# Recurrence output written in place in slots of 32 partitions, two units loaded ahead into the second activation tile, own tile for r*u*k

## The chip, the cores and the metric

One Trainium2 chip, one of its cores. The metric is the device time of one execution in microseconds (us), of which the median of several runs is given.

## What is computed

A recurrence per batch and head, and behind it two dense layers with their own activations:

```python
for t in range(S):                       # B, H, S, D = 4, 8, 768, 48
    cur = einsum('bhd,bhe->bhde', u * k[t], v[t])
    y[t] = einsum('bhd,bhde->bhe', r[t], state + cur)
    state = w[t][..., None] * state + einsum('bhd,bhe->bhde', k[t], v[t])
x = y as (3072, 384)
h = x @ w_in;  g = h - tanh(h);  x = g @ w_out          # 384 -> 2048 -> 384
h = x @ w_in2; s = h * softmax(h); x = layernorm(s) * g_ln @ w_out2   # 384 -> 1024 -> 384
```

The weights come as float64 and are converted on the chip into a high and a low part of f32 (tiles wa, wb); each dense product is three matmuls, low times high, high times low and high times high.

## The kernel before

**Recurrence.** The sequence of a batch is cut into NC = 6 chunks of 128 steps; batch times chunk gives 24 units. A unit is worked in stages: att_load (DMAs of w, r, k into rkw[u % 2], of v into vt[u % 4]), att_pre (range check of w on ScalarE, ACT; r*u*k on GpSimd, POOL; its sum per head on VectorE, DVE), att_0 (transposes of w and r on TensorE, PE; running product, scans of L274), att_1 (k scaled, L286 to L288), att_2 (q·k on PE, L301, masked into aq by L303; kt, the transpose of k), att_3 (state update: ds on PE, L317 and L318; st on DVE), att_4 (y). The heads stand in pairs j = 0..3: head 2j on partitions 0 to 47, head 2j+1 on 64 to 111.

In att_4, y of pair j lies in p[:, j] on the same partitions: 48 rows of each head, 16 left free. There are two calls with the state (L340, not in the first unit of a sequence) and two with aq (L343) per pair. Pairs 0 to 2 are copied (high part by ACT, L345, low part by DVE, L347) into the activation tile xs of the block; pair 3 goes to x3 (L346, L348) and from there by six DMAs (L351) into the free rows of xs. load_w1 puts the rows of w_in in the same order by four DMAs.

r*u*k is written to self.ruk, which is a view of inv; inv is also written by L286 and read by L288.

**Dense layers.** Six blocks of 512 columns (four units each), 16 steps m in each: part1 (L381, nine matmuls into hp, then the activation on ACT, DVE, POOL) and, two steps later, part2 (L405, nine matmuls into x2p). In block 0 each step also converts a pair of weight tiles (conv_a: raw loads by load_w1 and load_w2, then L121 to L135; two raw tiles in turn). xs[0] and xs[1] serve the blocks in turn. Then comes the third layer (L462, L544), which the change doesn't touch.

**Order.** The kernel writes work in a chosen order: a list `first` of stages of units 0 to 3 and of the first two conversions, sorted by keys (stage number plus 2.1 per unit), and then one loop over the steps s of all blocks, into which the later units' stages are placed. A planner orders the instructions of each engine's queue by that order as priority and by its own estimate of when each is ready; every queue then runs in its order. All DMAs are issued by SyncE (SP).

Of the kernel before, what the change touches and what calls it, by code (L numbers as in the profile page):

```python
# [20 lines left out]
C = 128  # L21
NC = S // C
# [36 lines left out]
class Kern:  # L59
# [101 lines left out]
    def att_setup(self, att, xp0, xp1):  # L161
        nc = self.nc
        rkw = att.tile([128, 2 * 3 * H * 64 + 32], F32, name="rkw")
        self.rkw = [x.rearrange("p (i h d) -> p i h d", i=3, h=H) for x in (rkw[:, 0:RKW], rkw[:, RKW:2 * RKW])]
        self.grp = [rkw[:, ROW * i:ROW * (i + 1) + 32] for i in range(3)]
        self.nat = rkw[:, 3 * ROW + 32:2 * RKW + 32].rearrange("p (i h d) -> p i h d", i=2, h=H)
        self.vt = [att.tile([128, DM], F32, name=f"vt{i}") for i in range(4)]
        self.inc = [att.tile([128, 4, C + 1], F32, name=f"inc{i}") for i in range(2)]
        self.rh = [att.tile([128, 4, C], F32, name=f"rh{i}") for i in range(2)]
        self.kh = [att.tile([128, 4, C], F32, name=f"kh{i}") for i in range(2)]  # L170
        self.inv = att.tile([128, 4, C], F32, name="inv")
        self.aq = att.tile([128, 2, 4, C], F32, name="aq")
# [12 lines left out]
        for t in self.st:
            nc.gpsimd.memset(t, 0.0)

    def att_load(self, u):
        nc = self.nc
        b, c = divmod(u, NC)  # L190
        t = self.rkw[u % 2]
# [3 lines left out]
        nc.sync.dma_start(  # L195
            out=self.vt[u % 4].rearrange("p (h d) -> p h d", h=H),
            in_=self.v[b, :, sl, :].rearrange("h p d -> p h d"),
        )

# [10 lines left out]
    def load_turned(self, u):  # L210
# [7 lines left out]
        for i, src in ((0, self.r), (1, self.k)):  # L218
            nc.sync.dma_start(out=self.nat[:, i], in_=src[b, :, sl, :].rearrange("h p d -> p h d"))
        nc.sync.dma_start(  # L220
            out=self.vt[u % 4].rearrange("p (h d) -> p h d", h=H),
            in_=self.v[b, :, sl, :].rearrange("h p d -> p h d"),
        )
        self.load_grp(0, u)
# [12 lines left out]
    def att_pre(self, u):  # L237
        nc = self.nc
        t = self.rkw[u % 2]
# [5 lines left out]
        nc.vector.reduce_sum(self.dg[u % 2].rearrange("p e j -> p j e"), self.ruk.rearrange("p (j e) d -> p j e d", e=2), axis=AX)  # L245

# [63 lines left out]
    def att_3(self, u):  # L310
# [5 lines left out]
        for j in range(4):  # L316
            self.mm(p[0:64, j], kn[:, j, 0:64], vt[:, 2 * j * D:2 * j * D + D], start=True, stop=True)  # L317
            self.mm(p[64:NP, j], kn[:, j, 64:NP], vt[:, (2 * j + 1) * D:(2 * j + 2) * D], start=True, stop=True)  # L318
        old, new, inc = self.st[u % 2], self.st[(u + 1) % 2], self.inc[u % 2]
        for e in range(2):  # L320
            s = slice(64 * e, 64 * e + D)
            n = new[s, :, s]
            end = inc[s, :, C:C + 1].to_broadcast([D, 4, D])
            if u % NC == 0:
                v.tensor_tensor(n, p[s], end, ALU.mult)
            else:
                v.tensor_tensor(n, p[s], old[s, :, s], ALU.add)
                v.tensor_tensor(n, n, end, ALU.mult)

    def att_4(self, u):  # L330
# [242 lines left out]
def fast_path(tc, K, const):  # L573
# [108 lines left out]
def general_path(tc, K, const):  # L682

    nc, v = tc.nc, tc.nc.vector
    with tc.tile_pool(name="g_dram", bufs=1, space=bass.MemoryType.DRAM) as dram:
# [23 lines left out]
        with (  # L709
# [166 lines left out]
```

## Time and profile before

| what | value |
|---|---|
| median of 3 runs | 778.8 us (777.76 to 779.06) |
| profiled execution, own time | 782.14 us |
| its span, first to last instruction | 780.3 us |
| mean granted clock of PE | 0.985 |
| PE busy | 731.3 us, 94% of the span |
| DVE busy | 582.5 us, 75% |
| ACT busy | 495.0 us, 63% |
| POOL busy | 419.7 us, 54% |
| DMA queue of the kernel | 112.19 MB, 55.5% of 16 engines' span |

Busy time is that of instructions under way, and matmuls overlap each other, so a busy PE is not PE at its peak. A wait is put down to the operation that came last. Times of rows are from the start of the span.

### The profile page before, as it was taken

The page shows a single profiled execution, that of the slowest core. Times are in us where ns is not written, and L with a number is a line of the kernel's source. Part 1 is how long each engine was busy: PE and PEld are TensorE (multiplying, and loading weights), DVE is VectorE, ACT ScalarE, POOL GpSimd, SP SyncE. Part 2 cuts the span into 40 slices and gives each one's busy share as a digit, 9 for nine tenths or more (in the row PEclk, how much of TensorE's full clock was granted, in tenths as well). Part 3 has the DMA queues.
Part 4 walks back from the last instruction along what each step waited for, and adds up shares of the span by engine and source line. Part 5 has one row for each costly group of instructions (what it writes and reads, how often), then busy time and mean ns, then how long its engine had stood idle before and what let it go on. Part 6 is the DMA issues. An engine that isn't in the chain of part 4 may idle for free. (4 is left out here: it accounts for less than half of the span.)

```text
span 780.3 us, 13211 instructions
## 1 busy us (share of the span) xinstructions
PE 731.3 (94%) x4338; PEld 605.5 (78%) x4338; DVE 582.5 (75%) x1023; ACT 495.0 (63%) x944; POOL 419.7 (54%) x389
## 2 busy tenths in 40 slices
PE   3677989899999999999999999999999999999996
PEld 2565767678887888887887887887778999998986
DVE  4688989776776677766676765468569899999992
ACT  3434777487776777686777765697745554554552
POOL 3444657466565656646555655367425444545440
PEclk9978999999999999999999999999999999999999
DMA  9964674778587568657665630043035555645531
GB/s 164 184 101 116 132 179 122 169 176 206 127 182 184 137 152 184 172 145 205 158 158 162 178 88 25 25 143 121 5 130 184 178 172 168 195 161 171 184 108 46
DMA packets 178158, 113.12 MB, mean 145 GB/s; under 512 B 95520, under 2 KB 166816, under 8 KB 178080
## 3 DMA queue, kind: packets, MB, share of 16 engines
q1 hardware_dynamic: 178080, 112.19, 55.5%
q8 instruction: 36, 0.59, 0.3%
q14 instruction: 42, 0.34, 0.1%
HBM read 88.81 MB, written 20.97 MB: 141 GB/s over the span
## 5 line engine op out<-in xcount | busy, mean ns | idle before, releaser
L405 PE MATMUL x2p<-g,wa 128*128 128x512 f32 x864 | 223.9, 398 | 4.0 <-ACT g L395 2.8
L381 PE MATMUL hp<-xs,wa 128*128 128x512 f32 x864 | 216.9, 395 | 5.5 <-DVE y L392 5.0
L381 PEld LDWEIGHTS hp<-xs,wa 128*128 128x128 f32 x864 | 162.5, 190 | 43.1 <-POOL wa L135 7.0
L405 PEld LDWEIGHTS x2p<-g,wa 128*128 128x128 f32 x864 | 158.1, 188 | 42.6 <-issue 4.2
L398 POOL TENSOR_TENSOR g<-y,g 128x512 fp32r<-128x512 f32 x96 | 128.6, 1340 | 42.7 <-ACT g L395 33.3
L387 DVE TENSOR_TENSOR y<-hp,t 128x512 f32<-128x512 f32 x96 | 65.9, 687 | 81.3 <-ACT t L386 65.5
L393 ACT ACTIVATE q<-t,cst 128x512 f32<-128x512 f32 x96 | 69.4, 723 | 65.6 <-DVE y L392 65.1
L462 PE MATMUL h<-wb,x2s 128*128 128x512 f32 x432 | 103.8, 392 | 3.0 <-POOL x2s L451 1.4
L544 PE MATMUL o<-wb,ts 128*128 128x384 f32 x576 | 105.1, 336 | 1.0 <-POOL ts L523 1.0
L544 PEld LDWEIGHTS o<-wb,ts 128*128 128x128 f32 x576 | 100.8, 188 | 3.0 <-POOL ts L523 1.3
L462 PEld LDWEIGHTS h<-wb,x2s 128*128 128x128 f32 x432 | 80.6, 188 | 20.0 <-POOL x2s L451 1.9
L397 POOL TENSOR_SCALAR g<-y 128x512 fp32r<-128x512 f32 x64 | 40.3, 630 | 91.9 <-DVE y L392 65.4
L386 ACT ACTIVATE t<-hp 128x512 f32<-128x512 f32 x96 | 56.5, 589 | 26.1 <-PE hp L381 25.4
L523 POOL TENSOR_TENSOR ts<-tw,ts 128x512 fp32r<-128x512 f32 x44 | 57.9, 1339 | 7.5 <-ACT ts L522 7.4
L392 DVE SCALAR_TENSOR_TENSOR y<-q,y 128x512 f32<-128x512 f32 x64 | 49.9, 780 | 4.4 <-ACT q L390 1.2
L451 POOL TENSOR_TENSOR x2s<-x2s 128x384 fp32r<-128x384 f32 x24 | 24.9, 1040 | 49.9 <-ACT x2s L450 49.9
L495 ACT ACTIVATE e<-so 128x1024 f32<-128x1024 f32 x24 | 25.5, 1060 | 37.2 <-DVE so L494 37.2
L390 ACT ACTIVATE q<-t,cst 128x512 f32<-128x512 f32 x64 | 46.2, 722 | 1.2
L519 DVE STREAM_TRANSPOSE tw<-sw 128x1024 f32<-128x1024 f32 x22 | 45.0, 2046 | 2.6 <-DMA sw<-dso 2.4
L286 POOL TENSOR_TENSOR inv<-inc,kh 112x512 f32<-112x512 f32 x24 | 29.7, 1236 | 32.0 <-ACT kh L278 25.9
L135 POOL TENSOR_TENSOR wa<-cv_x,wa 128x768 fp32r<-128x768 f32 x16 | 29.4, 1839 | 29.7 <-ACT wa L134 29.7
L301 PEld LDWEIGHTS qk<-rh,kh 48*128 48x128 f32 x384 | 28.0, 200 | 18.8 <-issue 12.3
(134 smaller groups left out, 1208.1 us busy)
## 6 DMA issues: line engine op xcount, KB each, us to landing
raw<-in_moe_w_out_dram SPq DMA_DIRECT2D x48, 384.0 KB, 4.4
dso<-so SPq DMA_DIRECT2D x22, 512.0 KB, 3.0
sw<-dso SPq DMA_DIRECT2D x88, 128.0 KB, 3.0
raw<-in_moe_w_in_dram SPq DMA_DIRECT2D x64, 144.0 KB, 3.6
rkw<-in_r_dram SPq DMA_DIRECT2D x64, 96.0 KB, 2.7
rkw<-in_k_dram SPq DMA_DIRECT2D x64, 96.0 KB, 2.5
rkw<-in_w_dram SPq DMA_DIRECT2D x64, 96.0 KB, 3.3
raw<-in_moe_w_in_dram SPq DMA_DIRECT2D x16, 384.0 KB, 3.6
```

The source lines that it names most:

```text
L381: self.mm(hp, self.wa[:, a, m, j * 128:(j + 1) * 128], xs[:, b, j], start=n == 0, stop=n == len(seq) - 1)
L386: nc.scalar.activation(t, hp, AF.Square)
L387: v.tensor_tensor(y, hp, t, ALU.mult)
L390: nc.scalar.activation(p, t, AF.Square, bias=self.c_fsb, scale=F_S)
L392: self.last_dve = v.scalar_tensor_tensor(y, p, F_E, y, ALU.add, ALU.mult)
L393: self.last_act = nc.scalar.activation(q, t, AF.Relu, bias=self.c_t2, accum_out=self.flags[:, col:col + 1])
L398: g.tensor_tensor(gs[:, 1], y, gs[:, 0], ALU.subtract)
L405: self.mm(self.x2p[d], self.wa[:, a, m, sl], gs[:, b], start=m == 0 and n == 0, stop=m == NM - 1 and n == 2)
L462: self.mm(p[:, f], xs[:, a, j], w, start=q == 0, stop=q == 8)
L519: self.turned = nc.vector.transpose(x.rearrange("p k (t b) -> p b k t", b=4), sw)
L523: nc.gpsimd.tensor_tensor(ts[:, 1, k], x[:, k], ts[:, 0, k], ALU.subtract)
L544: self.mm(p, ts[:, a, k], self.wb[:, b, k, DM:], start=q == 0, stop=q == 3 * NM2 - 1)
```

## The change

The eight heads' 384 rows of y are laid out as three column blocks i of 32 rows in each of the four partition groups 32j, feature 96j + 32i + row, so that xs is written by one copy and one subtraction of 128 partitions; x3 and the six DMAs are gone. The state is kept dense (2 x 48 columns per pair), v is loaded into a tile of 112 columns per pair with head 2j+1 at column 64 (two DMAs), and y is made of calls with 32 output rows: seven per pair, four in the first unit of a sequence. load_w1 puts w_in in the new row order (four DMAs); the old one stays for the general path. Units 2 and 3 are loaded into the memory of xs[1], which is requested as xs[1] only at unit 4; all four units' loads are issued before the first raw loads of weights, which are issued before the list `first`; the first two conversions stand at keys 4.15 and 6.25 instead of 0 and 2. For units 0 to 4, r*u*k and the scratch of the range check have tiles of their own.

```diff
-        self.vt = [att.tile([128, DM], F32, name=f"vt{i}") for i in range(4)]
+        self.vt = [att.tile([128, 4, NP], F32, name=f"vt{i}") for i in range(4)]
-        self.st = [att.tile([128, 4, NP], F32, name=f"st{i}") for i in range(2)]
+        self.st = [att.tile([128, 4, 2 * D], F32, name=f"st{i}") for i in range(2)]
-        self.x3 = xp0.tile([128, 2, C], F32R, name="x3")
-        self.xs = [xp.tile([128, 2, KM, BLK], F32R, name=f"xs{i}") for i, xp in enumerate((xp0, xp1))]
+        self.xs = [xp0.tile([128, 2, KM, BLK], F32R, name="xs0")]
+        self.xp1 = xp1
+        x = xp1.tile([128, 2 * RKW], F32, tag="xs1", name="rkw23")
+        self.rkw += [x[:, RKW * i:RKW * (i + 1)].rearrange("p (i h d) -> p i h d", i=3, h=H) for i in range(2)]
+        for t in self.vt:
+            nc.gpsimd.memset(t[:, :, D:64], 0.0)
...
+    def load_v(self, u):
+        b, c = divmod(u, NC)
+        v = self.v[b].rearrange("(j e) p d -> e p j d", e=2)
+        for e in range(2):
+            self.nc.sync.dma_start(out=self.vt[u % 4][:, :, 64 * e:64 * e + D], in_=v[e, c * C:(c + 1) * C])
...
     def att_pre(self, u):
+        ruk = self.ruk
+        if u <= UB:
+            ruk = self.gp.tile([128, BLK], F32, tag="y", name="ruk")[:, 0:DM].rearrange("p (h d) -> p h d", h=H)
         if u < TURN:
-            self.check_w(u, t[:, 2, :, 0:D], self.ruk)
-        nc.gpsimd.tensor_tensor(self.ruk, r, self.ub, ALU.mult)
-        nc.gpsimd.tensor_tensor(self.ruk, k, self.ruk, ALU.mult)
+            w = self.gp.tile([128, BLK], F32, tag="q", name="cw")[:, 0:DM].rearrange("p (h d) -> p h d", h=H) if u < UB else ruk
+            self.check_w(u, t[:, 2, :, 0:D], w)
+        nc.gpsimd.tensor_tensor(ruk, r, self.ub, ALU.mult)
+        nc.gpsimd.tensor_tensor(ruk, k, ruk, ALU.mult)
...
     def att_4(self, u):
+        terms = [] if first else [(i, None, 32 * i) for i in range(KM)]
+        terms = sorted(terms + [(0, 0, 0), (1, 0, 32), (1, 1, D), (2, 1, 80)], key=lambda t: t[0])
+        for n, (i, e, o) in enumerate(terms):
+            for j in range(4):
+                lhs, rhs = (st[:NP, j, o:o + 32], rh[:NP, j]) if e is None else (vt[:, j, o:o + 32], self.aq[:, e, j])
+                self.mm(p[32 * j:32 * j + 32, i], lhs, rhs, start=all(t[0] != i for t in terms[:n]),
+                        stop=all(t[0] != i for t in terms[n + 1:]))
+        if u == UB:
+            self.xs.append(self.xp1.tile([128, 2, KM, BLK], F32R, tag="xs1", name="xs1"))
+        xs = self.xs[blk % 2]
+        nc.scalar.copy(xs[:, 0, :, cols], p[:, 0:KM])
+        v.tensor_tensor(xs[:, 1, :, cols], p[:, 0:KM], xs[:, 0, :, cols], ALU.subtract)
+
+    def load_w1(self, raw, m):
+        dst = raw.rearrange("p (i f) two -> p i (f two)", i=KM)
         for j in range(4):
-            if not first:
-                for e, m in ((0, 64), (1, D)):
-                    self.mm(p[64 * e:64 * e + m, j], st[:NP, j, 64 * e:64 * e + m], rh[:NP, j], start=True, stop=False)
-            for e, m in ((0, 64), (1, D)):
-                h = 2 * j + e
-                self.mm(p[64 * e:64 * e + m, j], vt[:, h * D:h * D + m], self.aq[:, e, j], start=first, stop=True)
-        nc.scalar.copy(x3[:NP, 0], p[:NP, 3])
-        v.tensor_tensor(x3[:NP, 1], p[:NP, 3], x3[:NP, 0], ALU.subtract)
-        for j in range(KM):
-            for dst, src in ((48, 16 * j), (112, 64 + 16 * j)):
-                nc.sync.dma_start(out=xs[dst:dst + 16, :, j, cols].bitcast(F32), in_=x3[src:src + 16].bitcast(F32))
+            self.nc.sync.dma_start(
+                out=dst[32 * j:32 * j + 32], in_=wi[96 * j:96 * j + 96].rearrange("(i x) f -> x i f", i=KM)
+            )
...
     K.att_load(1)
+    K.att_load(2)
+    K.att_load(3)
...
-    first += [(SK * (u - 2) + 1.05, K.att_load, u) for u in range(2, UB + 2)] + [(SK * UB - 1, K.att_pre, UB)]
-    first += [(2.0 * m, lambda m: K.conv_a(cv, cvr, m), m) for m in range(early)]
+    first += [(SK * (u - 2) + 1.05, K.att_load, u) for u in range(UB, UB + 2)] + [(SK * UB - 1, K.att_pre, UB)]
+    K.raws = {m: K.load_pair(cvr, m) for m in range(early)}
+    first += [(4.15 + 2.1 * m, lambda m: K.conv_a(cv, cvr, m), m) for m in range(early)]
```

## Rows read from the trace of the kernel before

**Rows 1.** Busy time in three stretches; after the length each engine's busy us (instructions).

```profile
core 0: us, PE busy (x) PEld busy (x) DVE busy (x) ACT busy (x) POOL busy (x), PEclk, DMA share, GB/s
13.40:66.70 53.30, 33.18 (x332) 27.34 (x332) 38.81 (x77) 21.18 (x47) 22.58 (x20) 0.87 0.81 142
66.70:161.90 95.20, 85.51 (x498) 65.92 (x497) 81.99 (x168) 67.22 (x127) 57.10 (x42) 0.96 0.63 150
161.90:500.00 338.10, 337.75 (x2175) 271.78 (x2175) 230.36 (x412) 239.21 (x492) 197.73 (x193) 1.00 0.60 150
```

**Rows 2.** Timeline of PE, q·k of two successive units in the saturated part.

```profile
187.45 1.16 PE L301 MATMUL qk<-rh,kh 48*128 48x128 f32 x16
...
208.06 1.16 PE L301 MATMUL qk<-rh,kh 48*128 48x128 f32 x16
```

**Rows 3.** Timeline, units 0 to 3: start us, length us, engine, line, operation.

```profile
0.94 0.32 POOL L181 MEMSET rkw<- 128x256 f32 x1
...
7.14 1.00 POOL L243 TENSOR_TENSOR inv<-rkw,ub 128x384 f32<-128x384 f32 x1 [2.95 <-ACT inv L234]
...
15.82 0.56 DVE L129 TENSOR_SCALAR cv_a<-raw 128x384 uint32<-128x384 uint32 x1 [2.29 <-DMA raw<-in_moe_w_in_dram]
...
18.79 0.69 DVE L287 TENSOR_TENSOR tp<-kh,tp 112x512 f32<-112x512 f32 x1
...
20.75 2.08 PE L301 MATMUL qk<-rh,kh 48*128 48x128 f32 x16
...
31.33 0.39 SPq L194 DMA_DIRECT2D rkw<-in_k_dram  x1
...
39.13 0.56 DVE L245 TENSOR_REDUCE dg<-inv 128x8 f32<-128x384 f32 x1 [3.29 <-POOL inv L244]
```

**Rows 4.** Waits of DVE from 13.4 to 66.7 us: total us, times, longest.

```profile
DVE cv_a L129 <- DMA raw<-in_moe_w_in_dram: 5.2, 2, 2.9
```

**Rows 5.** Busy time and DMA in the first 20 us (columns as in rows 1).

```profile
0.00:20.00 20.00, 6.61 (x26) 4.72 (x27) 9.25 (x30) 6.87 (x12) 7.71 (x20) 1.00 0.99 166
```

**Rows 6.** Timeline from unit 3's last copy to the first part1.

```profile
62.97 0.28 DVE L348 TENSOR_TENSOR x<-x2p,x 112x128 fp32r<-112x128 f32 x1
...
63.31 3.78 SPq L351 DMA_DIRECT2D xs<-x  x6
...
64.24 1.34 DVE L303 COPY_PREDICATED aq<-mask,qk 128x512 f32<-128x512 uint8 x2 [0.99 <-PE qk L301]
...
65.48 1.01 DVE L129 TENSOR_SCALAR cv_a<-raw 128x384 uint32<-128x384 uint32 x2
...
66.73 1.65 PE L381 MATMUL hp<-xs,wa 128*128 128x512 f32 x3
```

**Rows 7.** SP's issue of the six DMAs per unit: ns min, median, max.

```profile
L351 SPq DMA_DIRECT2D xs<-x x144: 585/592/1387, 34.0 to 491.6; - x144
```

**Rows 8.** Waits of DVE in block 0 (first row), then its timeline at 80 us.

```profile
DVE cv_a L129 <- DMA raw<-in_moe_w_in_dram: 6.1, 2, 4.7
...
80.48 3.78 SPq L351 DMA_DIRECT2D xs<-x  x6
...
80.80 1.01 DVE L131 CUSTOM_DVE_ANT_0 cv_x<-raw,cv_a 128x768 uint16<-128x768 uint16 x2
...
85.00 0.52 SPq L361 DMA_DIRECT2D raw<-in_moe_w_in_dram  x1
```

**Rows 9.** Timeline of PE, eight transposes over the whole array, clock 1.0.

```profile
55.79 1.04 PE L260 MATMUL tp<-ident,rkw 128*128 128x128 f32 x8
```

**Rows 10.** Timeline of PE through ds and y of one unit in the saturated part.

```profile
318.05 0.26 PE L317 MATMUL ds<-vt,kn 128*64 128x48 f32 x1
...
318.45 0.30 PE L340 MATMUL y<-rh,st 112*48 112x128 f32 x1
318.49 0.22 PE L317 MATMUL ds<-vt,kn 128*64 128x48 f32 x1
...
320.02 0.47 PE L343 MATMUL y<-aq,vt 128*48 128x128 f32 x4
320.42 0.96 PE L405 MATMUL x2p<-g,wa 128*128 128x512 f32 x3
```

More of the change, by code (lines that the diff above doesn't have):

```diff
@@ L186, in att_setup, with rk @@
             nc.gpsimd.memset(t, 0.0)
+        for t in self.vt:
+            nc.gpsimd.memset(t[:, :, D:64], 0.0)
+    def rk(self, u):
+        return self.rkw[u if u < UB else u % 2]
     def att_load(self, u):
@@ L190, in att_load @@
         b, c = divmod(u, NC)
-        t = self.rkw[u % 2]
+        t = self.rk(u)
         sl = slice(c * C, (c + 1) * C)
@@ L194, in att_load @@
             nc.sync.dma_start(out=t[:, i, :, 0:D], in_=src[b, :, sl, :].rearrange("h p d -> p h d"))
[L195 to L198, printed above, removed]
+        self.load_v(u)
+    def load_v(self, u):
[3 more added lines that the diff above has]
+            self.nc.sync.dma_start(out=self.vt[u % 4][:, :, 64 * e:64 * e + D], in_=v[e, c * C:(c + 1) * C])
     def load_grp(self, i, u):
@@ L219, in load_turned @@
             nc.sync.dma_start(out=self.nat[:, i], in_=src[b, :, sl, :].rearrange("h p d -> p h d"))
[L220 to L223, printed above, removed]
+        self.load_v(u)
         self.load_grp(0, u)
@@ L259, in _transposes @@
         for j in range(4):
-            self.nc.tensor.transpose(p[:, j], self.rkw[u % 2][:, i, 2 * j:2 * j + 2, :], self.ident)
+            self.nc.tensor.transpose(p[:, j], self.rk(u)[:, i, 2 * j:2 * j + 2, :], self.ident)
         return p
@@ L316, in att_3 @@
         for j in range(4):
-            self.mm(p[0:64, j], kn[:, j, 0:64], vt[:, 2 * j * D:2 * j * D + D], start=True, stop=True)
-            self.mm(p[64:NP, j], kn[:, j, 64:NP], vt[:, (2 * j + 1) * D:(2 * j + 2) * D], start=True, stop=True)
+            self.mm(p[0:64, j], kn[:, j, 0:64], vt[:, j, 0:D], start=True, stop=True)
+            self.mm(p[64:NP, j], kn[:, j, 64:NP], vt[:, j, 64:NP], start=True, stop=True)
         old, new, inc = self.st[u % 2], self.st[(u + 1) % 2], self.inc[u % 2]
@@ L321, in att_3 @@
             s = slice(64 * e, 64 * e + D)
-            n = new[s, :, s]
+            cs = slice(D * e, D * e + D)
+            n = new[s, :, cs]
             end = inc[s, :, C:C + 1].to_broadcast([D, 4, D])
@@ L326, in att_3 @@
             else:
-                v.tensor_tensor(n, p[s], old[s, :, s], ALU.add)
+                v.tensor_tensor(n, p[s], old[s, :, cs], ALU.add)
                 v.tensor_tensor(n, n, end, ALU.mult)
@@ L336, in att_4, with load_w1g @@
         first = u % NC == 0
-        for j in range(4):
-            if not first:
-                for e, m in ((0, 64), (1, D)):
-                    self.mm(p[64 * e:64 * e + m, j], st[:NP, j, 64 * e:64 * e + m], rh[:NP, j], start=True, stop=False)
-            for e, m in ((0, 64), (1, D)):
-                h = 2 * j + e
-                self.mm(p[64 * e:64 * e + m, j], vt[:, h * D:h * D + m], self.aq[:, e, j], start=first, stop=True)
-        xs, x3 = self.xs[blk % 2], self.x3
-        nc.scalar.copy(xs[:NP, 0, :, cols], p[:NP, 0:3])
-        nc.scalar.copy(x3[:NP, 0], p[:NP, 3])
-        v.tensor_tensor(xs[:NP, 1, :, cols], p[:NP, 0:3], xs[:NP, 0, :, cols], ALU.subtract)
-        v.tensor_tensor(x3[:NP, 1], p[:NP, 3], x3[:NP, 0], ALU.subtract)
-        for j in range(KM):
-            for dst, src in ((48, 16 * j), (112, 64 + 16 * j)):
-                nc.sync.dma_start(out=xs[dst:dst + 16, :, j, cols].bitcast(F32), in_=x3[src:src + 16].bitcast(F32))
-    def load_w1(self, raw, m):
+        terms = [] if first else [(i, None, 32 * i) for i in range(KM)]
[11 more added lines that the diff above has]
+    def load_w1(self, raw, m):
+        wi = self.w_in.bitcast(U32)[:, m * 256:(m + 1) * 256]
+        dst = raw.rearrange("p (i f) two -> p i (f two)", i=KM)
+        for j in range(4):
+            self.nc.sync.dma_start(
+                out=dst[32 * j:32 * j + 32], in_=wi[96 * j:96 * j + 96].rearrange("(i x) f -> x i f", i=KM)
+            )
+        return raw
+    def load_w1g(self, raw, m):
         wi = self.w_in.bitcast(U32)[:, m * 256:(m + 1) * 256]
@@ L371, in conv_a @@
     def conv_a(self, pool, rpool, m):
-        raw = self.load_pair(rpool, m)
+        raw = self.raws.pop(m, None)
+        if raw is None:
+            raw = self.load_pair(rpool, m)
         self.convert(pool, raw, self.wa[:, 0, m], self.wa[:, 1, m], bank=self.ps_a)
@@ L716, in general_path @@
             for m in range(NM):
-                for load, out in ((K.load_w1, w1[:, :, m * 128:(m + 1) * 128]), (K.load_w2, w2[:, m])):
+                for load, out in ((K.load_w1g, w1[:, :, m * 128:(m + 1) * 128]), (K.load_w2, w2[:, m])):
                     K.to_f32(rp, load(rp.tile([128, DM, 2], U32, tag="raw", name="raw"), m), out)
```

4 lines of the change are left out of this document (2 added, 2 removed).

## The prediction

> **What bounds the kernel now.** I read the busy times in long stretches first, then what VectorE (DVE) waited for in the stretch where TensorE (PE) starves, then single instructions there, and last the recurrence's stretch inside the long saturated part.
>
> The stretches [rows 1] show three regimes. From 161.9 to 500 us PE is busy 337.75 of 338.1 us: nothing but less PE work shortens it. The start of q·k of two successive units lies 20.61 us apart there [rows 2], so four steps of part1 and part2 and one unit of the recurrence fill PE without a gap. Between 66.7 and 161.9 us (block 0, where the weights are still being converted) DVE is busiest for its kind of work, 81.99 of 95.2 us; PE is busy 85.5, but with matmuls that stand in line for DVE. Before 66.7 us PE has only the recurrence of units 0 to 4; DVE is busy 38.81 of the 53.3 us from 13.4 on, so 14.5 us of it are idle. What an early us is worth: it moves the point from which PE is never idle again, and so the end, unless block 0 eats it.
>
> **The start, units 0 to 3.** The reader is to see one queue effect in [rows 3]. DVE is done with unit 1's scan by 13.5 us, then comes the conversion of w_in and w_out for m = 0 (L129) ahead of unit 0's L287, and it waits for its raw load: the row at 15.82 us carries 2.29 us of idle time, and L287 starts at 18.79, q·k of unit 0 at 20.75. The second effect: unit 3's k is issued at 31.33 us, because its place in rkw is unit 1's and because raw loads stand ahead on SP; and r*u*k shares the tile inv, which L288 of the unit before still reads. DVE's L245 at 39.13 us pays 3.29 us for both.
>
> The change moves the loads of units 2 and 3 (8 DMAs, now 10, v being split in two) ahead of gl and of the raw loads of m = 0 and 1, and the conversions behind units 0 and 1 (keys 4.15 and 6.25 instead of 0 and 2). So the waits of DVE on raw data, 5.2 us [rows 4], and the one on r*u*k, 3.3 us, lose their cause: 8.5 us. What is late next: raw 0 itself. Four units are 16 loads of 192 KB, 3.15 MB; at the 166 GB/s of the first 20 us [rows 5] they are through at about 2 + 19 = 21 us, raw 0 (0.79 MB, 4.7 us) at 26, raw 1 at 31. By the order of keys DVE reaches conversion 0 after unit 1's q·k; unit 0 runs undisturbed from 13.4 us, some 10 us of DVE work and waits lie between, so it gets there at 24 to 25. I charge 2 us (0 if the planner that orders each engine's queue puts other work there, 5.2 as the whole old wait if it doesn't). It is an estimate.
>
> The move passes nothing on POOL; eight extra memsets (pads of the second rkw pair and of vt), at most 0.32 us each by the widest like them, come ahead of POOL's first product, which had waited 2.95 us for ACT [rows 3]: 2.6 us at most, hidden. The second activation tile is requested only at unit 4; it has to wait for the readers of units 2 and 3, which are done by then, because unit 4's y lies behind unit 3's on PE and ACT. If that cover were gone, ACT's copy of unit 4 would stand, with the conversions behind it.
>
> **Rows written in place.** Of each unit go: ACT's copy of the fourth pair, DVE's L348 (0.28 us, [rows 6]) and six DMAs on SP at 0.592 us each [rows 7], 3.55 us, with the wait ahead of them. Units 0 to 3 give 4 x 0.28 = 1.1 us of DVE. On the path that sets the start of block 0 the tail goes too [rows 6]: L348 starts at 62.97, the six DMAs at 63.31, part1 at 66.73. In those 3.5 us DVE did other work (L303 of unit 4, 1.34 us, and L129 twice, 1.01 us), which then falls behind the start of part1. So part1 starts about 8.5 - 2 + 1.1 + 2.35 = 10 us sooner, near 57, but only 7.6 us of that is DVE work really advanced.
>
> In block 0 DVE idles 13.2 us, 6.1 of it on raw w_in data [rows 8]. One cause is on show there: the conversion that frees a raw tile (L131) starts at 80.80 us and takes 1.01, but SP stands in the six DMAs from 80.48 on, has a load of k behind them, and issues the next raw load at 85.00. Without them it goes out 3 us or so sooner. Four units pass in block 0; two raw tiles in turn hide part of each delay. I take half of the 6.1 us, 3, between 0 and 6.1, and 4 x 0.28 = 1.1 us for L348. After block 0 SP's waits delay nothing that PE waits for, so the removed DMAs are worth nothing there. load_w1 keeps four DMAs; v has one more per unit, under half a us of SP.
>
> **PE's own cost.** This is where the change could lose. A unit's y takes 16 calls now (8 in a sequence's first unit), 28 after (16 in a first one). f32 calls run as two instructions: [rows 9] has eight f32 instructions of 128 columns, one stream, in 1.04 us, 0.11 apart ((1.04 - 0.27)/7). In [rows 10] y needs 318.45 to 320.33, 1.8 us, for 32 such instructions, 0.055 apart. So outputs at partitions 0 to 63 and at 64 to 111 already run side by side, each stream at 0.11. They also run apart from each other: L340 of the 48-wide stream starts at 318.45, before the last L317 of the 64-wide one at 318.49, which stands ahead of it in the program. After the change four outputs of 32 partitions are four streams of 7 calls: 7 x 2 x 0.11 = 1.54 us. The issue can keep up: 56 instructions in 1.54 us are 0.0275 apart, and the 16 instructions of ds from 318.05 to 318.49 are 0.028 apart (0.44/16). So -0.25 us for each later unit, 0 for a first one (4 x 0.22 = 8/2 x 0.22). Against that stands a change of shape between ds (64 wide) and y (32 wide), which are neighbours here; the nearest row is the change from L343 to L405, about 0.1 us from 320.33 to 320.42, and up to 0.2 with the slower first matmul. I take 0.15. Net -0.1 us for 14 later units in the saturated part: -1 us, between -3.5 (no price of the change of shape) and, with two streams only, 14 x (28 - 16) x 0.11 + 2 x 8 x 0.11 = +20.
>
> The Trainium skill, page TensorE: Matmul & The Clock Gate, Part 3, says that matmuls start and end strictly in program order. By that rule the two instructions of one call would block the queue behind them, and only the second of a call could overlap the first of the next: 28 x 0.11 = 3.1 us for y. The trace disagrees by the start at 318.45 above. The Trainium skill, page TensorEngine Tiling (Array Packing), Key Properties, also says that a change of tiling mode drains the engine; the 0.1 us agrees.
>
> **The sum.** Start: -8.5 + 2 - 1.1 = -7.6 us. Block 0: -3 - 1.1 = -4.1. PE: -1. Together -12.7, say -13. The profiled execution's own time is 782.1 us (span 780.3), which becomes 769; it lies 0.4% over the median of 778.8 us, from which the forecast follows: 766 us.
>
> **The rivals.**
> (a) As summed, 755 to 774: chance 0.60.
> (b) Slower. Four streams of f32 don't run at once: no row shows more than two, and two streams at 0.11 already take one column in 0.055 us. Then y is 3.1 us, +20 us in the saturated part (+1.32 us for each of 14 units, +0.88 for two), and -13 + 20 = +7: 786 us, with up to 5 more where block 0 has no PE time left, so 780 to 792. It decides the sign from about 2.7 us per y on (13/14 us over today's 1.8). For it: a third stream is unseen, and a strict order of the instructions would give the same time (the rule of the Trainium skill quoted above, from TensorE: Matmul & The Clock Gate, would do this). Against it: the independent streams of [rows 10], and that ds already issues at the rate needed. Chance 0.15.
> (c) The gain at the start is absorbed. The planner orders the queues by its own estimate; if it puts conversions ahead of unit 0 again, or block 0 is held by the cadence of raw loads, only L348 (2.2 us) and PE's 1 us stay: 775.5, so 774 to 780. The change would then not do what it says. For it: the 13.2 us of DVE idleness in block 0 could take up any shift. Chance 0.15.
> (d) More: block 0 gives back most of its idleness as well, some 6 us more, and the tail at 63 to 66.7 counts in full: 740 to 755. Chance 0.10.
>
> **How the numbers follow.** Likeliest is (a), 766 us. 752 to 780 takes in (a) nearly whole, (c), and half of (d); it leaves out (b) and the lower end of (d), two in ten. A measurement of this kernel can't tell less than about 0.2% from no change, 1.6 us: 777.2 to 780.4. Faster: (a), (d) and half of (c), 0.78. Same: half of (c), 0.07. Slower: (b), 0.15.
>
> **What the profile after would show.** Right: q·k of unit 0 near 15 us instead of 20.75; no wait of DVE on raw data before unit 0's L287; unit 3's y ahead of part1 by under 2 us; part1 near 57 us; y in the saturated part in 1.55 to 1.7 us with two q·k 20.5 apart. Wrong: y over 2.7 us and a distance of 21.9 us (rival b); part1 at 57 us but the first stretch without PE gaps still near 162 (rival c); DVE's wait on raw 0 over 5 us.

## The result, and the profile after

The changed kernel takes 772.97 us (median of 9, 768.49 to 775.33), the kernel before beside it 780.61 (777.76 to 782.8): 0.9888 of it, 95% interval 0.9864 to 0.9912. It was timed a second time beside the later experiments: 774.38, 0.9905 (0.9875 to 0.9934). So it is about 1% faster (1.1% and 1.0%); 1.6% had been forecast (766 us, range 752 to 780). The profiled execution of after has a span of 773.4 us against 780.3. A profile is one execution, and a few lie off the median of their kernel (changed 775.22 us against 772.97, rows only 782.88 against 777.82, scaling held 766.63 against 769.7, both cures with r*u*k shared 773.57 against 770.37), so that two or three us between the times of two profiles prove little.

The same three stretches of after as in [rows 1]; columns as there:

```profile
13.40:66.70 53.30, 36.55 (x474) 29.43 (x476) 38.40 (x79) 22.88 (x45) 21.30 (x19) 0.81 0.77 134
66.70:161.90 95.20, 83.33 (x551) 63.21 (x544) 83.96 (x159) 66.87 (x124) 59.18 (x44) 0.96 0.62 157
161.90:500.00 338.10, 338.10 (x2569) 273.20 (x2568) 230.22 (x400) 242.49 (x485) 199.89 (x195) 1.00 0.54 145
```

DVE's first stretch is no denser than before (38.40 us against 38.81), though its old waits are gone. The timeline of after shows why: the first row is q·k of unit 0, the rows from 35.28 to 45.00 us are where unit 2's state update stands, the last four are the first part1 and the end of block 0 (start us, length us, engine, line, operation, idle time before it and what ended it). L121 scales a raw tile, L319 copies kt into kn, L328 is ds, L339 the state; L401 is part1, L135 the last operation of a conversion.

```profile
12.52 1.23 PE L312 MATMUL qk<-rh,kh 48*128 48x128 f32 x8
...
35.28 1.87 SPq L367 DMA_DIRECT2D raw<-in_moe_w_in_dram  x4
35.90 1.01 PE L318 MATMUL x2p<-ident,kh 112*128 112x112 f32 x4
37.19 0.43 SPq L384 DMA_DIRECT2D raw<-in_moe_w_out_dram  x1
...
42.51 0.88 ACT L121 ACTIVATE raw<-raw 128x768 uint32<-128x768 uint32 x1 [2.41 <-DMA raw<-in_moe_w_out_dram]
43.29 0.51 ACT L319 COPY kn<-x2p 128x448 f32<-128x448 f32 x1
43.85 0.34 PE L328 MATMUL ds<-vt,kn 128*64 128x48 f32 x1 [6.95 <-ACT kn L319]
...
45.00 0.74 DVE L339 TENSOR_TENSOR st<-ds,st 48x192 f32<-48x192 f32 x2 [4.52 <-PE ds L329]
...
55.31 0.73 PE L401 MATMUL hp<-xs,wa 128*128 128x512 f32 x2 [0.59 <-ACT xs L359]
60.23 3.00 PE L401 MATMUL hp<-xs,wa 128*128 128x512 f32 x8
...
155.44 1.84 POOL L135 TENSOR_TENSOR wa<-cv_x,wa 128x768 fp32r<-128x768 f32 x1 [0.26 <-ACT wa L134]
157.34 2.37 PE L401 MATMUL hp<-xs,wa 128*128 128x512 f32 x9 [0.43 <-POOL wa L135]
```

q·k of unit 0 starts at 12.52 us instead of 20.75 [rows 3], 8.2 us sooner. Then a new wait: the scaling of raw 2 stands in ACT's queue ahead of kn of unit 2, and waits for a load that SP issued at 35.28 to 37.2 us, behind the loads of w, r and k of units 4 and 5. kt was ready at 36.9; kn came at 43.29, ds at 43.85, and DVE lost 4.52 us at L339. part1 starts at 55.31 (66.73 in [rows 6]), but with two matmuls only; its bulk follows at 60.23, behind q·k of unit 4, where the kernel before has 18 matmuls in one row from 66.73 on:

```profile
66.73 5.97 PE L381 MATMUL hp<-xs,wa 128*128 128x512 f32 x18
```

So the first matmul comes 11.4 us sooner and the bulk 6.5. The last row of the fence above is the one that counts: block 0 ends when part1 of m = 15 gets its weights from POOL's L135. That is at 157.34 us; before, it was 161.9.

DVE's waits of after, the first row from 13.4 to 66.7 us, the other three in block 0 (55.3 to 157.3 us): total us, times, longest.

```profile
DVE cv_a L129 <- DMA raw<-in_moe_w_in_dram: 0.8, 1, 0.8
...
DVE aq L314 <- PE qk L312: 4.1, 3, 2.2
DVE y L407 <- ACT t L406: 3.0, 3, 1.3
...
DVE cv_a L129 <- DMA raw<-in_moe_w_in_dram: 0.2, 1, 0.2
```

DVE's raw waits are nearly gone in both places (0.8 us after 5.2 in [rows 4], 0.2 after 6.1 in [rows 8]); in block 0, waits on PE and ACT stand in their place.

y of one unit in the saturated part, between ds and part2:

```profile
312.74 0.28 PE L328 MATMUL ds<-vt,kn 128*64 128x48 f32 x2
312.94 0.43 PE L354 MATMUL y<-rh,st 112*32 112x128 f32 x8
313.19 0.41 PE L354 MATMUL y<-aq,vt 128*32 128x128 f32 x8
313.41 0.40 PE L354 MATMUL y<-rh,st 112*32 112x128 f32 x8
313.63 0.62 PE L354 MATMUL y<-aq,vt 128*32 128x128 f32 x16
314.07 0.41 PE L354 MATMUL y<-rh,st 112*32 112x128 f32 x8
314.29 0.41 PE L354 MATMUL y<-aq,vt 128*32 128x128 f32 x8
314.62 0.73 PE L425 MATMUL x2p<-g,wa 128*128 128x512 f32 x2
```

56 instructions in 1.6 us; eight take 0.22, so they start 27 ns apart on average. The single records show them by fours, one on each group of columns: 6 to 7 ns apart within a four, 0.09 to 0.13 us from one four to the next. These are four streams at once, each as fast as one alone in [rows 9].

Put together, the span's -6.9 us, with the forecast beside it:

| stretch | before | after | change | forecast |
|---|---|---|---|---|
| 13.4 us to part1 of m = 15, DVE busy | 120.8 | 118.5 | -2.3 | -2.2 (eight L348) |
| the same, DVE idle | 27.7 | 25.4 | -2.3 | -9.5 |
| part1 of m = 15 to the last part2 | 415.7 | 411.2 | -4.5 | -1 |
| last part2 to the end | 202.7 | 204.9 | +2.2 | 0 |

That DVE's busy time fell by just the forecast 2.2 us is chance. Busy time holds stalls: DVE's products of the state with a column of inc (L340, before L328) take 0.35 us as a rule, but some of the ten in this stretch take up to 1.9 (see the last section). What goes beyond 0.35 us each is 3.2 us before and 5.2 after, 0 in loads only, 2.9 to 5.7 in the other variants below. Without it, busy time is 117.6 us before and 113.4 after: the eight L348 are 2.2 us of the 4.3, and most of the rest is work that falls outside the stretch (more of unit 0 is done by 13.4 us, one operation of part1 less before m = 15).

### The profile page after: what moved, and what is told of

Its sections match the earlier page's. It is cut to its first block, busy times and chain, and to the rows that moved or that the text cites. A ratio compares the mean times of both kernels' runs of the same rounds, so it can differ in the third digit from the quotient of the medians.

```text
span 773.4 us, 13992 instructions
## 1 busy us (share of the span) xinstructions
PE 725.0 (94%) x4882; PEld 599.2 (77%) x4882; DVE 585.2 (76%) x999; ACT 490.8 (63%) x920; POOL 419.0 (54%) x397
## 4 chain that ended last, share of the span: by engine, by line
PE 49%; DVE 28%; ACT 10%; DMA 5%; SPq 4%; issue 3%; POOL 1%; ACTq 0%; DVEq 0%; POOLq 0%
PE hp L401 19%; PE x2p L425 19%; DVE tw L539 6%; DVE so L514 4%; PE y L354 4%; DVE e L508 4%; DMA raw<-in_moe_w_out_dram 3%; ACT e L515 3%; DVE part L504 3%; PE qk L312 3%; SPq L367 2%; PE o L564 2%; DVE cv_x L131 2%; SPq L201 1%; PE kt L318 1%
## 5 line engine op out<-in xcount | busy, mean ns | idle before, releaser
L401 PE MATMUL hp<-xs,wa 128*128 128x512 f32 x864 | 216.0, 395 | 2.5 <-POOL wa L135 1.3
L401 PEld LDWEIGHTS hp<-xs,wa 128*128 128x128 f32 x864 | 163.4, 190 | 39.7 <-POOL wa L135 2.3
L407 DVE TENSOR_TENSOR y<-hp,t 128x512 f32<-128x512 f32 x96 | 65.8, 686 | 76.8 <-ACT t L406 60.4
L417 POOL TENSOR_SCALAR g<-y 128x512 fp32r<-128x512 f32 x64 | 40.3, 630 | 81.5 <-DVE y L412 77.4
L515 ACT ACTIVATE e<-so 128x1024 f32<-128x1024 f32 x24 | 25.5, 1061 | 59.6 <-DVE so L514 59.6
L543 POOL TENSOR_TENSOR ts<-tw,ts 128x512 fp32r<-128x512 f32 x44 | 55.9, 1292 | 4.4 <-ACT ts L542 4.4
L412 DVE SCALAR_TENSOR_TENSOR y<-q,y 128x512 f32<-128x512 f32 x64 | 51.4, 803 | 2.9
L517 POOL TENSOR_TENSOR st<-st,cst 128x1 f32<-128x1 f32 x23 | 12.6, 549 | 53.0 <-DVE st L498 45.3
L121 ACT ACTIVATE raw<-raw 128x768 uint32<-128x768 uint32 x24 | 21.8, 908 | 27.9 <-DMA raw<-in_moe_w_out_dram 24.3
```

The lines of the kernel that those rows point to most:

```text
L401: self.mm(hp, self.wa[:, a, m, j * 128:(j + 1) * 128], xs[:, b, j], start=n == 0, stop=n == len(seq) - 1)
L407: v.tensor_tensor(y, hp, t, ALU.mult)
L412: self.last_dve = v.scalar_tensor_tensor(y, p, F_E, y, ALU.add, ALU.mult)
L515: nc.scalar.activation(e, so, AF.Square, accum_out=va)
L543: nc.gpsimd.tensor_tensor(ts[:, 1, k], x[:, k], ts[:, 0, k], ALU.subtract)
```

## The experiments

All are variants of the changed kernel unless said otherwise. m = 0 and m = 15 are the starts of part1, its first matmul, in the profiled execution (in before, rows only, shared r*u*k and the kernel with both cures 18 matmuls start there, in the changed kernel, scaling held, raw 2, 3 first, six DMAs put back and the two with g first only two, and the bulk comes 5 to 6 us later); DVE is busy and idle from 13.4 us to part1 of m = 15; the ratio is to the kernel before on the same chip.

| kernel | m = 0 | m = 15 | DVE busy | DVE idle | ratio |
|---|---|---|---|---|---|
| before | 66.7 | 161.9 | 120.8 | 27.7 | 1 |
| changed | 55.3 | 157.3 | 118.5 | 25.4 | 0.9888 |
| changed, again | 56.3 | 156.8 | 118.5 | 24.9 | 0.9905 |
| rows only | 67.3 | 167.0 | 118.4 | 35.2 | 0.9941 |
| loads only | 66.1 | 163.0 | 114.7 | 34.9 | 1.0046 |
| shared r*u*k | 59.9 | 156.8 | 119.5 | 23.9 | 0.9852 |
| scaling held | 51.4 | 151.2 | 116.9 | 20.9 | 0.9841 |
| raw 2, 3 first | 54.1 | 152.6 | 117.7 | 21.6 | 0.9845 |
| raw 2, 3 first, one held, shared | 61.8 | 157.2 | 119.6 | 24.2 | 0.9837 |
| six DMAs put back | 59.7 | 173.0 | 121.0 | 38.6 | 1.0062 |
| less conversion | 51.5 | 141.4 | 102.5 | 25.5 | 0.9664 |
| g first | 57.2 | 153.4 | 116.1 | 23.9 | 0.9805 |
| g first, scaling held | 52.6 | 156.9 | 119.4 | 24.1 | 0.9877 |

**The two halves apart.** Rows only: the loads, the conversions' keys and r*u*k as before. Loads only: y in its old layout, with x3 and its six DMAs.

```diff
 rows only
-    K.att_load(2)
-    K.att_load(3)
-    K.raws = {m: K.load_pair(cvr, m) for m in range(early)}
-    first += [(4.15 + 2.1 * m, ...conv_a...)]
+    first += [(2.0 * m, ...conv_a...)]
 loads only
-        nc.scalar.copy(xs[:, 0, :, cols], p[:, 0:KM])
+        nc.scalar.copy(x3[:NP, 0], p[:NP, 3])
+        for j in range(KM):
+            for dst, src in ((48, 16 * j), (112, 64 + 16 * j)):
+                nc.sync.dma_start(out=xs[dst:dst + 16, ...], in_=x3[src:src + 16]...)
...
```

> Rows of y in place alone: the new att_4, vt, st and load_w1, but units 2 and 3 loaded into rkw[u % 2] after units 0 and 1, conversions at keys 0 and 2, r*u*k in inv, all as before. Theory (the gain of 7.6 us is the sum of about 3.5 us from the start, carried by the early loads, and about 4 us from PE and the missing copies): q.k of unit 0 stays near 20.75 us, part1 of block 0 starts 2 to 4 us sooner than 66.7 because the six DMAs behind unit 3 are gone, distance of q.k in the saturated part 20.4 us on average; total -3.5 to -5.5 us, ratio 0.993 to 0.9955. Rival 1 (everything is in the rows): 0.989. Rival 2 (everything is in the loads, PE gains nothing): 0.998 to 1.0.

> Early loads alone: y, x3, its copies and the six DMAs as before; units 2 and 3 in the second activation tile, all loads ahead of the weights, conversions at 4.15 and 6.25, r*u*k with its own tile. Theory: q.k of unit 0 at 12.5 us as in the changed kernel, ACT stands again some us for raw data of m = 2 with unit 2's kn behind it, part1 near 60 us or a little later since the six DMAs come back; DMAs of x3 also delay the raw loads. Total -2 to -4 us, ratio 0.995 to 0.9975. Rival 1: the loads carry all, 0.989. Rival 2: they carry nothing because block 0 takes it up, 0.999 to 1.001.

Measured: rows only 0.9941 (0.9912 to 0.997), as expected. In its profiled execution part1 of m = 15 comes at 167.0 us, 5 later than before, and what lies behind it is 4.2 us shorter (614.2 us against 618.4), on PE. That execution took 782.88 us, as long as the profiled one of before (782.14), so its long block 0 can't stand for the median of 777.82, and how long block 0 is there, no trace shows. Loads only 1.0046 (1.0022 to 1.0069), a loss where a gain was expected. Together they gain about 1%, more than the sum of the two. SP's queue in loads only shows the link:

```profile
33.59 1.07 SPq L201 DMA_DIRECT2D vt<-in_v_dram  x1
34.77 4.31 SPq L363 DMA_DIRECT2D xs<-x  x6
39.19 0.52 SPq L373 DMA_DIRECT2D raw<-in_moe_w_in_dram  x1
```

With unit 0 early, its six DMAs stand at 34.77 us ahead of the loads of raw 2, which go out at 39.19 instead of 35.28. By the views of waits to 66.7 us ds waits 12.6 us on kn there (10.2 in the changed kernel).

What lengthened block 0 in that execution of rows only is seen in its timeline (L393 is part1; L121 and L407, the copy g, on ACT; L417 is part2), and in the busy times of the stretch behind it:

```profile
136.72 2.35 PE L393 MATMUL hp<-xs,wa 128*128 128x512 f32 x9
140.73 0.89 ACT L121 ACTIVATE raw<-raw 128x768 uint32<-128x768 uint32 x1 [2.72 <-DMA rkw<-in_w_dram]
141.53 0.60 ACT L407 CAST g<-y 128x512 fp32r<-128x512 f32 x1
142.18 4.29 PE L417 MATMUL x2p<-g,wa 128*128 128x512 f32 x9 [3.11 <-ACT g L407]
...
142.10:153.40 11.30, 11.22 (x34) 8.48 (x35) 6.54 (x12) 4.78 (x9) 8.11 (x6) 0.50 0.75 172
```

A raw tile's scaling waits, g waits behind it, PE waits 3.11 us for g, and then runs 11.3 us at a granted clock of 0.50 (1.2 GHz): nine matmuls in 4.29 us, where the nine at 136.72 took 2.35.

**The six DMAs alone.**

```diff
+        for j in range(KM):
+            for o in (48, 112):
+                nc.sync.dma_start(out=self.x3d[...], in_=xs[o:o + 16, :, j, cols].bitcast(F32))
```

> The changed kernel with six DMAs per unit put back on SP, behind y's subtraction as before the change (16 partitions, 256 columns each, from xs into a scratch in DRAM that nobody reads), so that SP again waits for DVE there and issues for 3.55 us, with raw loads behind them. Nothing waits for them. The prediction's step (without them raw loads go out sooner, which is worth 3 us in block 0, between 0 and 6.1): part1 of m = 15 comes 3 to 6 us later, 0.992 to 0.999 of the kernel before. Rival (in the changed kernel SP waits 45 us in block 0 for DVE to free raw tiles, so the six DMAs fit into time in which it waits anyway): part1 of m = 15 within 2 us of 157, 0.986 to 0.993.

Measured: 1.0062 (1.0037 to 1.0087), 13 us slower than the changed kernel. Both expectations were too small. SP's queue, the scaling of raw 2, and the totals of the first 66.7 us (from 13.4):

```profile
35.55 5.05 SPq L363 DMA_DIRECT2D x3d<-xs  x6
40.71 1.93 SPq L370 DMA_DIRECT2D raw<-in_moe_w_in_dram  x4
...
45.91 0.88 ACT L121 ACTIVATE raw<-raw 128x768 uint32<-128x768 uint32 x1 [5.67 <-DMA raw<-in_moe_w_out_dram]
...
PE ds L328 <- ACT kn L319: 14.7, 2, 11.1
...
DVE cv_a L129 <- DMA raw<-in_moe_w_in_dram: 8.9, 4, 3.5
```

The last row is from 66 to 165 us; in block 0 of the changed kernel this wait is 0.2. raw 2 is issued 5.4 us later than in the changed kernel, and its scaling is 3.4 us later. DVE's idle time grows from 25.4 to 38.6 us. So raw loads do limit the first 160 us once the start is early, and what the row layout takes off SP is what makes the early loads pay. The 13 us are the price of these copies, which go to a scratch in DRAM; in loads only, which has the old six, DVE's idle time is 34.9 us, 9.5 more than in the changed kernel instead of 13.2.

**r*u*k in inv again.**

```diff
-        if u <= UB:
-            ruk = self.gp.tile([128, BLK], F32, tag="y", name="ruk")...
-            w = self.gp.tile([128, BLK], F32, tag="q", name="cw")...
-            self.check_w(u, t[:, 2, :, 0:D], w)
+            self.check_w(u, t[:, 2, :, 0:D], ruk)
```

> The changed kernel with r*u*k and the range check back in inv; all else as changed. Theory: in the start r*u*k of a unit waits again for L288 of the unit before, but DVE comes to the sum in order anyhow, so 0 to 2 us: ratio 0.989 to 0.9915. Rival (the own tile is what made unit 0 and 1 flow): part1 5 us or more later, ratio 0.994 or more.

Measured: 0.9852 (0.9818 to 0.9886), below both expectations and not slower than with the tile of its own. The first matmul of part1 comes 3.6 to 4.6 us later, but now 18 stand in one row, and the bulk starts no later than the 60.23 us of the changed kernel:

```profile
59.94 5.97 PE L398 MATMUL hp<-xs,wa 128*128 128x512 f32 x18
```

part1 of m = 15 comes no later either: the tile buys two early matmuls and nothing behind them.

**The new wait, cured in two ways.** The ACT work of conversions 2 and 3 queued behind ACT's copy of unit 3; or the loads of raw 2 and 3 issued ahead of those of units 4 and 5.

```diff
 scaling held
+        with self.tc.issue_after(self.copy3.ins) if m in (2, 3) else nullcontext():
             self.convert(pool, raw, self.wa[:, 0, m], self.wa[:, 1, m], bank=self.ps_a)
 raw 2, 3 first
+        self.raws[u - 2] = self.load_pair(self.cvr, u - 2)
+        with self.tc.issue_after(self.last_raw.ins):
+            self.att_load(u)
```

> The changed kernel, with ACT's work of conversions 2 and 3 (scaling of the raw low words, cast) queued behind ACT's copy of unit 3's y; nothing else. In the changed kernel ACT stands 2.4 us at 42.5 us for the raw load of m = 2 while kn of unit 2, ready at 36.9 us, is behind it, and PE's ds waits 6.95 us for kn. Theory (this new wait gives back a part of what the start gained): ds of unit 2 at about 40.5 us instead of 43.85, part1 3 to 5 us sooner, total 2 to 4 us less than the changed kernel, ratio 0.984 to 0.9865. Rival (block 0 is held by its own cadence of conversions, so an earlier start is not worth anything): part1 sooner but ratio 0.988 to 0.990.

> The changed kernel, but SP issues the loads of raw 2 and raw 3 ahead of those of units 4 and 5, so that ACT's scaling of raw 2, which stands ahead of kn of unit 2 in ACT's queue, finds its data sooner. Raw 0 is free at about 31 us; with the 2.3 us of issue and the 4.7 us until the last load of raw 2 landed in the changed kernel, its data is there at 38 us instead of 42.5, a us after kt (36.9). Theory (the wait on raw 2 took part of the gain at the start): the wait of ds on kn falls from 10.2 to 6 us or less, part1 starts by 52 us, 0.983 to 0.987 of the kernel before. Rival (units 4 and 5, loaded later, are then late themselves, or conversion 2 was never what the start hung on): part1 at 55 us or later, 0.988 or more.

Measured: 0.9841 (0.9806 to 0.9875) and 0.9845 (0.9817 to 0.9872); part1 of m = 15 comes 6.1 and 4.7 us sooner than in the changed kernel's profile, of which 1.6 and 0.9 us are less DVE busy time and 4.5 and 3.8 less idle time; by the ratios the two cures are worth 3.4 to 5 us of the whole. The total of ds on kn, from 10.2 us, in the one and in the other:

```profile
PE ds L328 <- ACT kn L319: 7.0, 2, 4.0
...
PE ds L333 <- ACT kn L324: 6.9, 2, 4.6
```

In the second this wait missed the 6 us expected, and part1 of m = 0 (54.1) the 52; the time was met. Both cures (the hold for conversion 3 alone, `if m == 3`) with r*u*k in inv again:

> The changed kernel with the loads of raw 2 and 3 ahead of those of units 4 and 5, the work of ACT for conversion 3 behind ACT's copy of unit 3, and r*u*k and the range check in inv again. If the two waits of ACT on raw data (raw 2 ahead of kn of unit 2, raw 3 ahead of the copy of unit 3) are separate costs, their removal adds up: part1 by 51 us or sooner (51.4 and 54.1 with one of them removed), part1 of m = 15 by 151, 0.976 to 0.984 of the kernel before. If both cure the same us: that of the better one, 0.984 to 0.987.

Measured: 0.9837 (0.9807 to 0.9868), inside the range, but not as expected: part1 starts at 61.8 us (18 matmuls in a row; the bulk comes at 56.8 with the scaling held and at 59.3 with raw 2, 3 first), not by 51. The gains don't add up.

**DVE's work.** L130, one of DVE's three operations per half tile, left out of block 0's conversions.

```diff
+            if bank is None:
                 v.scalar_tensor_tensor(a, H_[:, s], 0xC0000000, a, ALU.bitwise_and, ALU.bitwise_or)
```

> The changed kernel without L130, which puts the sign and the top exponent bit back, in block 0's conversions: 2 x 0.555 us less of DVE for each m, 15.5 us in block 0 and 2.2 us before it. The weights come out without signs, so the values are other ones; PE, ACT and POOL do the same work. Theory (block 0 is held by DVE's work, and only shifts when the start is earlier): from part1 of m = 0 to that of m = 15 it takes 92 us or less instead of 102, and 0.965 to 0.978 of the kernel before. Rival (raw loads, POOL's subtraction or the order on PE hold block 0's length): 98 us or more there, and 0.984 or more, which is what the start alone could give.

Measured: 0.9664 (0.9636 to 0.9692). From 13.4 us to part1 of m = 15, the changed kernel first, then this one:

```profile
13.40:157.30 143.90, 115.99 (x1001) 89.76 (x999) 118.54 (x230) 85.57 (x160) 78.85 (x61) 0.91 0.67 147
...
13.40:141.40 128.00, 108.58 (x996) 85.70 (x995) 102.53 (x199) 83.88 (x159) 77.98 (x61) 0.92 0.76 167
```

DVE's busy time falls by 16.0 us, the stretch by 15.9, and the idle time stays at 25.5. So up to here DVE sets the pace: its work plus the waits that its queue meets.

**g ahead of the scaling in block 0.** ACT's work of conversion m queued behind its copy g of step m - 3; and the same with the hold of the start.

```diff
+        with self.tc.issue_after(self.gc[0, m - 3].ins) if m >= 4 else nullcontext():
             self.convert(pool, raw, self.wa[:, 0, m], self.wa[:, 1, m], bank=self.ps_a)
```

> The changed kernel with ACT's work of conversion m (from 4 on) queued behind ACT's copy g of step m - 3. There, in five places of block 0, ACT's scaling of a raw tile waits 1.4 to 3.4 us for its load with the copy g of a step right behind it, and part2 of that step behind g; PE's waits on g are 7.9 us in block 0, and part2 at 82.13 runs at half the clock after one of them. Theory (in block 0 the time goes where raw waits stand on ACT ahead of g): PE's waits on g fall to 4 us or less, part1 of m = 15 comes 3 to 7 us sooner than 157.3, 0.979 to 0.986 of the kernel before. Rival (DVE's work alone sets block 0, and ACT's waits only lie beside it; a scaling that is put later only makes its conversion later): part1 of m = 15 at 156 or later, 0.987 or more.

> As the run before, and also the hold of the start: ACT's work of conversions 2 and 3 behind its copy of unit 3 (0.9841 by itself). If the two places are separate, both gains add up: part1 by 52 us, that of m = 15 by 148, 0.973 to 0.980. If block 0 takes back what the start gives: 0.981 to 0.986.

Measured: the first 0.9805 (0.9777 to 0.9833), with part1 of m = 15 at 153.4, 3.9 us sooner; PE's waits on g from 55.3 to 157.3 us, first in the changed kernel, then here:

```profile
PE x2p L425 <- ACT g L415: 7.9, 6, 2.0
...
PE x2p L426 <- ACT g L416: 4.3, 2, 2.4
```

It is the fastest complete kernel of the study, 767.5 us, though its interval overlaps those of the two cures. Not all of the 3.9 us is shown to come from g: DVE's idle time is 1.5 us less, its busy time 2.4, and 2.3 of that are shorter state products (2.9 us beyond 0.35 each instead of 5.2), which moved with the order. With the hold as well it was 0.9877 (0.9844 to 0.991): the two don't add up either, and the second expectation's upper end was passed. Its start is 4.6 us sooner than without the hold, then a step at 71 us loses this:

```profile
71.53 1.65 PE L428 MATMUL x2p<-g,wa 128*128 128x512 f32 x3 [5.30 <-ACT g L418]
72.98 3.63 PE L404 MATMUL hp<-xs,wa 128*128 128x512 f32 x9
```

PE waits 5.30 us on g and then works at a granted clock of 0.50 to 73.0 us and of 0.59 to 76.6 (nine matmuls in 3.63 us).

**The order of y's calls.** The seven terms of pair 0, then those of pair 1, and so on.

```diff
-        for n, (i, e, o) in enumerate(terms):
-            for j in range(4):
+        for j in range(4):
+            for n, (i, e, o) in enumerate(terms):
```

> The changed kernel with y's calls in another order: all seven terms of pair 0, then of pair 1 and so on, instead of the four pairs in turn. Calls and results are the same. Theory (a call waits only for those of its own 32 columns, and calls behind it may start, but only a few of them): four calls in turn are needed for the four streams; with pairs one after another most of the 28 calls of y run in one stream, 28 x 0.22 = 6.2 us less what overlaps at three borders, so 4 to 6 us instead of 1.6, and 24 us or more between two q.k instead of 20.4; over 20 units 50 to 90 us more, 1.05 to 1.11 of the kernel before. Rival (any number of calls overtake): y stays at 1.6 us, and the time is that of the changed kernel within 0.3%.

Measured: 1.0548 (1.0511 to 1.0584), the lower half of what was expected. y of one unit, its first and last rows:

```profile
313.72 0.41 PE L354 MATMUL y<-rh,st 112*32 112x128 f32 x2
313.96 0.38 PE L354 MATMUL y<-aq,vt 128*32 128x128 f32 x2
...
318.44 0.38 PE L354 MATMUL y<-aq,vt 128*32 128x128 f32 x2
318.76 1.43 PE L425 MATMUL x2p<-g,wa 128*128 128x512 f32 x5
```

The same 56 instructions take 5.0 us instead of 1.6. One stream after another would be 28 x 0.22 = 6.2; overlap at the three borders of pairs gives 1.2 back (in the rows left out, eight instructions take 0.44 us there, where eight of one stream take 0.88). So calls overtook each other only near the borders, and the four streams need the four pairs in turn.

## Why the prediction was right in sign and short in size

**The start.** The causes named were the right ones: q·k of unit 0 is 8.2 us sooner, and DVE's raw wait fell to 0.8 us (2 had been charged for raw 0, on which DVE starts at 25.48 us, where 24 to 26 had been estimated). "What is late next: raw 0 itself" was the failing step. It was raw 2, whose loads stand on SP behind those of units 4 and 5, and it is not DVE that waits for it but ACT, with kn of unit 2 behind it. The prediction looked for the wait on DVE alone, and did not ask what stands behind ACT's L121. By the two cures it cost 4.7 and 6.1 us at part1 of m = 15 in the profiles, 3.4 to 5 us of the whole by the ratios. part1 at 55.3 us met the forecast of 57 by luck: only two matmuls stood there, and the bulk, at 60.2, is 6.5 us sooner where 10 had been forecast.

**r*u*k.** The 3.3 us were priced as a wait of DVE. With the tile only two matmuls come sooner, by about 4 us; the bulk and part1 of m = 15 don't, so the term in the sum was worth 0.

**L348.** Eight of them, 2.2 us, are gone. That DVE's busy time fell by 2.3 is no proof of the price: its state products took 2.0 us longer, and other work lies outside the stretch.

**Block 0.** Forecast -3 through SP, besides L348; measured, nothing that can be seen: from the bulk of part1 to m = 15 it is 97.1 us instead of 95.2 (102.0 from the first matmul). The raw waits of DVE did vanish, as said, but the queues met other waits (q·k, t), so a vanished wait was no gain. What would have been right is the table's reading: without the stalls of the state products, DVE's busy time up to part1 of m = 15 lies between 113.2 and 115.4 us in all the table's variants with whole conversions, the stalls (0 to 5.7 us) and the idle time (20.9 to 38.6) move, and the start's gain is not a gain until it shows at m = 15. Rival (c), "the gain at the start is absorbed", described half of what happened, and its range of 774 to 780 begins where the measurements lie (773.0 and 774.4). The six DMAs, on the other hand, were priced far too low for a kernel whose start is early: 3 us, where DVE's idle time grows by 9.5 us with the old six and by 13.2 with those put back. The prediction added the parts up; they are not additive.

**PE.** "Net -0.1 us for 14 later units" was right in its pieces: between q·k of units 8 and 23 y takes 24.1 us instead of 27.8 (0.25 less per unit, about as forecast) and ds 7.7 instead of 6.0, its change of shape (0.12 per unit, against 0.15). The sum was too small: those 15 units take 305.9 us instead of 310.9, 20.39 each instead of 20.73, and rows only has the same 20.39. Of the 5.0 us, y and ds are 2.0; q·k is 1.2 shorter, part1 0.9 and part2 0.8, for which the prediction had no term. They come with the rows: over the same 15 units q·k, part1 and part2 take 18.4, 125.4 and 128.4 us before, 18.4, 125.3 and 128.3 in loads only, 17.2, 124.5 and 127.5 in rows only. A part of it is that q·k is less often broken up: before, PE goes 21 times from part1 or part2 to q·k and 8 times from q·k to them, after 17 and 4 times. The rest has no cause that a run shows.

**Luck.** In the profiles, the start and block 0 gave 4.6 us where 11.7 had been forecast, and PE gave 4.5 where 1 had been. Without the 3.5 us by which PE gave more, the change would have come to 776 to 778 us, half the gain and in the middle of rival (c)'s range. That it came to 773.0 and 774.4, at the upper end of (a), is luck: no step of the prediction leads to these 3.5 us.

Rival (b), four streams not at once, is refuted: 1.6 us for y, not 3.1. The Trainium skill, page TensorE: Matmul & The Clock Gate, Part 3, has matmuls start and end strictly in program order, from which the prediction had worked out 3.1 us. The measurement decides against it for calls on different columns, while the run with pairs one after another shows that the order in which calls are written still counts.

**The end.** From the last part2 to the end both profiles of the changed kernel need 2.2 to 2.4 us more than before (204.9 and 205.1 against 202.7); its variants need 202.5 to 203.9. The third layer's code is unchanged. The traces show one operation of DVE there that is longer, L514 into so (128 x 1024, 23 times, 0.75 us at its shortest): 34.4 and 34.6 us in the two profiles of the changed kernel, 27.8 before, 28.1 to 33.4 in the variants, and every long one starts beside a running operation of POOL. The variants with most of it (32.1 to 33.4) end in 202.6 to 203.9 us, so it is not the whole cause; that stays open.

## What to carry to other kernels

When an engine's queue is fixed, look for every instruction in it that waits for a load, and at what stands right behind it: here a scaling on ACT held first kn, then g, and each time PE paid. Price an earlier start at the place where the stage ends, by the busy and idle time of the engine that paces it, not at the place where the stage begins. Parts of a change that share a queue (loads and row DMAs on SP) have no separate prices: one was worth -0.6%, the other +0.5%, both about -1%. Busy time is not work alone: set an operation's mean beside its shortest before a change in busy time is put down to a term of the sum.

## What the runs showed of the hardware

- Four f32 matmul streams of 32 output columns each, on different columns of the array, run at once at full pace (27 ns between instructions on average, against 0.11 us in one stream), if neighbouring calls are on different columns; with seven calls of one group in a row it is 5.0 us instead of 1.6.
- A PE wait of some us in block 0 was followed by a stretch at half pace: in rows only, 3.11 us of waiting and then 11.3 us at a granted clock of 0.50 (1.2 GHz), an estimated 5.6 us lost, more than by the wait itself.
- DVE's state products (L340, 48 x 192, both inputs in SBUF), 0.35 us as a rule, took 1.4 us each in the changed kernel at 68.16 us, beside two operations of POOL (fence below). No run changed this, but the 14 kept traces speak for POOL: all 346 products that start while POOL runs nothing take 0.34 to 0.36 us; of the 102 that start beside a running operation of POOL 94 take 0.52 to 1.97, and each of these ends 0.20 to 0.22 us after such an operation does. The 560 like operations with an input in PSUM (L337, L339) take 0.36 us at most, also the 133 of them beside POOL.

```profile
67.80 1.81 POOL L135 TENSOR_TENSOR wa<-cv_x,wa 128x768 fp32r<-128x768 f32 x1 [6.18 <-ACT wa L134]
68.16 2.83 DVE L340 TENSOR_TENSOR st<-st,inc 48x192 f32<-48x192 f32 x2
69.56 1.21 POOL L303 TENSOR_SCALAR_AFFINE_SELECT aq<-dg 128x1024 f32<-128x1024 f32 x1
```
